# Second phase: an expert's remainder slot comes first, and small remainders run in column tiles, by branches

## The chip, the cores and the metric

The kernel runs on one core of a Trainium2 chip. The metric is the device time of one execution in microseconds (us). The engines are TensorE (PE), VectorE (DVE), ScalarE (ACT), GpSimd (POOL) and SyncE (SP), which issues most transfers.

## The reference

Three stages, all in float32. Attention in chunks and a first MLP with a rational activation give 3072 rows of 512 numbers; the third stage, which the change touches, sends each row to one of 8 experts:

```python
def _moe2_ref(x, w_gate, w1, w2):          # x [3072, 512], w1 [8, 512, 1024], w2 [8, 1024, 512]
    logits = x @ w_gate
    expert_idx = np.argmax(logits, axis=1)
    ...
    gate_w = probs[np.arange(N), expert_idx]
    for e in range(E):
        mask = expert_idx == e
        ...
        h = np.maximum(xe @ w1[e], 0.0)
        ye = h @ w2[e]
        out[mask] = gate_w[mask, None] * ye
```

The inputs come from a fixed seed. Counted with the reference, experts 0 to 7 get 0, 647, 638, 266, 0, 568, 0 and 953 tokens. In slots of 128 tokens that is 0, 6, 5, 3, 0, 5, 0 and 8 slots, 27 in all, and the remainders (the tokens beyond whole slots) are 7 for expert 1, 126 for expert 2, 10 for expert 3, 56 for expert 5 and 57 for expert 7.

## The kernel before

The first phase (attention, first MLP, gate, a rank of each token within its expert) takes some 690 us. The rows leave it sorted by expert into a DRAM buffer xs_d, each with its gate weight and its row number in the output.

The second phase works through the sorted rows in slots of 128 tokens. The expert with the most tokens comes first (slots 0 to 7, expert 7), then experts 1, 2, 3 and 5 from slots 8, 14, 19 and 22. For each slot j there are these steps, each with a function of its own:

- sl_load(j): SP loads the slot's 128 rows. Its address is in tBi, a table that plan_b1 computes on VectorE.
- weights1, weights2: SP loads the raw weights of the slot's expert into r1 and r2, in transfers with a condition, so that they move data only where the expert changes.
- sl_xt (L769 to L773): four transposes on PE; ACT copies the result as the high half (fp32r), VectorE computes the low half, and copies gate weight and row number to gid.
- sl_mm1 (L783): 24 matmuls of 128x128 by 128x512, since high and low halves of x and w1 make three products. They use w1h and w1l, converted from r1.
- sl_relu (L790): ACT, two halves.
- sl_ht (L798 to L801): eight transposes on PE, then high halves on ACT and low halves on VectorE.
- sl_mm2 (L807 to L809): 24 matmuls with w2h and w2l, converted from r2.
- sl_out (L818 to L824): VectorE multiplies by the gate weight and computes the row index, and GpSimd scatters the rows to the output.

hilo (L750, L751) converts one quarter of a weight matrix, with one operation on ACT and one on VectorE. on_change(j, piece) does it for four quarters behind a branch on both engines (a register load, L760, and a jump, L761), where slot j's expert is a new one. For slots 2 and 3 the conversions stand without a branch.

The program order of one turn j of the loop, which each engine follows for its part, is: weights1(j+2), ht(j), conversion of w2 for j; weights2(j+1), mm1(j+1), relu(j+1), xt(j+2), load(j+3), conversion of w1 for j+2; mm2(j), out(j). From slot 23 on, the turns stand within branches on the number of slots (nt, loaded at L1199, compared at L1192), which each engine loads once. There is no other scheduler: engines wait for each other by semaphores only.

Of the kernel before, what the change touches and what calls it, by code (L numbers as in the profile page):

```python
# [47 lines left out]
def build(ctx: ExitStack, tc, q, k, v, w_in, w_out, a, b, w_gate, w1, w2, cst, out):  # L48
# [6 lines left out]
    def T(shape, name, dt=F32):  # L55
        return sb.tile(shape, dt, name=name)
# [46 lines left out]
    r1 = [cut(AT, 1024 * i, 1024) for i in range(4)]  # L103
    r2 = [cut(AT, 4096, 1024), cut(AT, 5120, 1024), cut(elf, 0, 1024), cut(elf, 1024, 1024)]
    hs = cut(elf, 2048, 1024)
    sx = [cut(AT, 6144, XW), X2[:, 0], X2[:, 2]]
    ys = X2[:, 1, 0:D]
    wif = WI.rearrange("p f h c -> p f (h c)")
# [540 lines left out]
    sA = T([128, E], "sA")  # L649
    tAi = T([128, 2], "tAi", I32)  # L650
    tBi = T([128, 4], "tBi", I32)
    p_t = T([128, 4, E], "p_t")
# [5 lines left out]
    p_v = T([128, 4], "p_v")  # L658
    p_w = T([128, 4], "p_w")
    p_pr = cut(XT, 0, E * E, (E, E))  # L660
    p_lb = T([128, 32], "p_lb", BF16)
# [6 lines left out]
    def bc(x, n):  # L668
        return x.unsqueeze(1).to_broadcast([128, n, E])
# [10 lines left out]
    def plan_b1():  # L680
        vt = nc.vector
        vt.tensor_scalar(out=p_nbi, in0=p_cnt, scalar1=127.0, scalar2=None, op0=ALU.add)
        vt.tensor_scalar(out=p_nbi, in0=p_nbi, scalar1=7, scalar2=None, op0=ALU.logical_shift_right)
        vt.tensor_copy(out=p_nb, in_=p_nbi)
        vt.tensor_tensor(out=p_pr, in0=bc(p_nb, E), in1=lowm, op=ALU.mult)
        vt.tensor_reduce(out=p_en, in_=p_pr, op=ALU.add, axis=AX.X)
        vt.tensor_tensor(out=p_st, in0=p_en, in1=p_nb, op=ALU.subtract)
        vt.tensor_tensor(out=p_t[:, 0], in0=p_st, in1=sA, op=ALU.mult)
        vt.tensor_reduce(out=p_v[:, 0:1], in_=p_t[:, 0], op=ALU.add, axis=AX.X)
        vt.tensor_scalar(  # L690
            out=p_t[:, 1], in0=iota_e, scalar1=tA[:, 1:2], scalar2=p_en[:, E - 1:E], op0=ALU.is_lt, op1=ALU.mult
        )
# [44 lines left out]
    def sl_w1(w, kk):  # L737
        ex, ch = w
        src = w1[bass.ds(ex, 1), 128 * kk:128 * kk + 128, :].rearrange("o p f -> (o p) f")
        nc.sync.dma_start(out=r1[kk], in_=src, cond=ch, bounds_check=None)  # L740

    def sl_w2(w, kk):
        ex, ch = w
        src = w2[bass.ds(ex, 1), 256 * kk:256 * kk + 256, :].rearrange("o (a p) f -> p (o a) f", a=2)
        nc.sync.dma_start(
            out=r2[kk].rearrange("p (a f) -> p a f", a=2), in_=src, cond=ch, bounds_check=None
        )

    def hilo(src, hi, lo):
# [29 lines left out]
    def sl_mm1(j, kk):  # L779
        xh, xl = sxh[j % 2], sxl[j % 2]  # L780
        for m, (w, x) in enumerate(((w1h, xh), (w1l, xh), (w1h, xl))):
            for c in range(2):
# [2 lines left out]
                    start=(kk == 0 and m == 0), stop=(kk == 3 and m == 2),  # L785
                )

    def sl_relu(j):
# [24 lines left out]

    ixb = [T([128, 1], f"ix{i}", I32) for i in range(2)]

    def sl_out(j):
        g = gid[j % 4]
        nc.vector.tensor_scalar(out=ys, in0=ACC[j % 2], scalar1=g[:, 0:1], scalar2=None, op0=ALU.mult)  # L818
        ix = ixb[j % 2]
        if j < 2:  # L820
            nc.vector.tensor_copy(out=ix, in_=g[:, 1:2].bitcast(I32))
        else:
            nc.vector.tensor_tensor(out=ix, in0=g[:, 1:2].bitcast(I32), in1=skip[:, j:j + 1], op=ALU.add)  # L823
# [12 lines left out]
    KV.append(eb.tile([128, 2, 2, 2, 8, 64], F32, name="KV"))  # L836
    scratch = [ACC[2]]

    mid = ExitStack()

    def middle():
        early.close()
# [3 lines left out]

    def switch():
        mid.close()
        lp = ctx.enter_context(tc.tile_pool(name="lp", bufs=1))
# [243 lines left out]
    assert not todo  # L1093


    i = NCH - 1
    for kk in (2, 3):
        sl_w2(Z["a"], kk)
# [22 lines left out]
        sl_mm2(0, c)  # L1121
    sl_out(0)
    sl_load(2)

    def weights1(j):
        Z[j] = sl_w(j)
        for kk in range(4):
            sl_w1(Z[j], kk)

    def weights2(j):  # L1130
        for kk in range(4):
            sl_w2(Z[j], kk)

    weights1(2)
    sl_load(3)
    sl_ht(1)
    for kk in range(4):
# [11 lines left out]
    for kk in range(4):  # L1149
        sl_mm1(2, kk)  # L1150
        if kk < 3:
            sl_s1(kk)
    sl_relu(2)
    sl_xt(3, XB[2])
    sl_load(4)
    sl_s1(3)


    def head(j):
        if j + 2 < NS:  # L1160
            weights1(j + 2)
        sl_ht(j)
        if j > 2:
            on_change(j, sl_s2)

    def ahead(j):
        weights2(j + 1)
        for kk in range(4):
            sl_mm1(j + 1, kk)
        sl_relu(j + 1)  # L1170
        if j + 2 < NS:
            sl_xt(j + 2, XB[2])
            if j + 3 < NS:
                sl_load(j + 3)
            on_change(j + 2, sl_s1)

    def done_(j):
        for c in range(8):
            sl_mm2(j, c)
        sl_out(j)  # L1180

    for j in range(2, NS0 - 1):
# [19 lines left out]

def consts():
    import numpy as np
    c = np.zeros((128, CST_W), np.float32)
# [10 lines left out]
    c[:, 176:240] = (e[None, :] <= e[:, None]).reshape(-1)  # L1216
    c[:, 240:368] = p[None, :] > p[:, None]
    return c


# [53 lines left out]
```

## Time and profile before

| | before |
|---|---|
| median of 3 runs | 1050.24 us (1049.44 to 1052.48) |
| the profiled execution, its time | 1046.15 us |
| its span, first to last instruction | 1044.4 us |
| PE busy | 989.3 us (95%) |
| DVE busy | 702.2 us (67%) |
| ACT busy | 616.1 us (59%) |
| mean granted clock of TensorE | 0.984 |

The span is what the trace shows; the rows below are in us from its start. The granted clock is a share of full speed. Busy times leave out register loads, branches and the issuing of transfers.

### The profile page before, as it was taken

The page shows a single profiled execution, that of the slowest core. Times are in us where ns is not written, and L with a number is a line of the kernel's source. Part 1 is how long each engine was busy: PE and PEld are TensorE (multiplying, and loading weights), DVE is VectorE, ACT ScalarE, POOL GpSimd, SP SyncE. Part 2 cuts the span into 40 slices and gives each one's busy share as a digit, 9 for nine tenths or more (in the row PEclk, how much of TensorE's full clock was granted, in tenths as well). Part 3 has the DMA queues.
Part 4 walks back from the last instruction along what each step waited for, and adds up shares of the span by engine and source line. Part 5 has one row for each costly group of instructions (what it writes and reads, how often), then busy time and mean ns, then how long its engine had stood idle before and what let it go on. Part 6 is the DMA issues. An engine that isn't in the chain of part 4 may idle for free. (4 is left out here: it accounts for less than half of the span.)

```text
span 1044.4 us, 18684 instructions
## 1 busy us (share of the span) xinstructions
PE 989.3 (95%) x6427; PEld 845.7 (81%) x6427; DVE 702.2 (67%) x1283; ACT 616.1 (59%) x1118; POOL 384.8 (37%) x412
## 2 busy tenths in 40 slices
PE   4678998999999999999999999998999999999996
PEld 3567886888888898898898888886888888888885
DVE  6899998887877777877877878968324425244421
ACT  2557776786777777777777778764324325234321
POOL 2456664543663453463453464542101000000010
PEclk9889998999999999999999999999999999999999
DMA  9756323221221121121121022022124133154311
GB/s 252 225 176 173 131 81 107 56 61 52 82 71 62 61 82 51 51 82 51 52 81 52 21 102 71 1 72 71 42 76 168 46 122 113 52 178 145 113 42 38
DMA packets 48395, 93.09 MB, mean 89 GB/s; under 512 B 6935, under 2 KB 15391, under 8 KB 48288
## 3 DMA queue, kind: packets, MB, share of 16 engines
q1 hardware_dynamic: 43312, 78.46, 24.9%
q0 software_dynamic: 4080, 12.61, 3.2%
q8 instruction: 53, 0.87, 0.3%
q10 hardware_dynamic: 896, 0.72, 0.3%
q14 instruction: 54, 0.44, 0.1%
HBM read 169.32 MB, written 15.50 MB: 177 GB/s over the span
## 5 line engine op out<-in xcount | busy, mean ns | idle before, releaser
L379 PE MATMUL bank<-XX,WI 128*128 128x384 f32 x1536 | 303.0, 346 | 4.4 <-DVE EL L395 2.5
L379 PEld LDWEIGHTS bank<-XX,WI 128*128 128x128 f32 x1536 | 269.1, 191 | 17.9 <-DVE EL L395 5.0
L389 POOL TENSOR_TENSOR EL<-EL 128x384 f32<-128x384 f32 x128 | 133.5, 1043 | 234.0 <-ACT EL L388 233.9
L423 POOL TENSOR_TENSOR GG<-EL,GG 128x384 fp32r<-128x384 f32 x128 | 131.7, 1029 | 79.1 <-ACT GG L422 36.3
L783 PE MATMUL bank<-WI,XX 128*128 128x512 f32 x648 | 155.5, 395 | 2.8 <-ACT XX L771 1.7
L783 PEld LDWEIGHTS bank<-WI,XX 128*128 128x128 f32 x648 | 119.4, 188 | 28.2 <-ACT XX L771 1.8
L824 POOL DMA_INDIRECT out_dram<-X,ix x27 | 29.4, 1087 | 294.9 <-DVE ix L823 278.9
L431 PE MATMUL bank<-WOa,GG 128*128 128x512 f32 x288 | 115.7, 402 | 0.0
L432 PE MATMUL bank<-WOa,GG 128*128 128x512 f32 x288 | 114.8, 398 | 0.0
L415 DVE SCALAR_TENSOR_TENSOR EL<-EL,ab 128x384 f32<-128x384 f32 x114 | 107.8, 946 | 3.3
L422 ACT CAST GG<-EL 128x384 fp32r<-128x384 f32 x128 | 65.3, 510 | 67.1 <-DVE EL L415 48.6
L387 ACT ACTIVATE EL<-bank 128x384 f32<-128x384 f32 x128 | 62.1, 485 | 68.5 <-PE bank L379 67.6
L413 DVE SCALAR_TENSOR_TENSOR EL<-EL 128x384 f32<-128x384 f32 x114 | 64.2, 563 | 53.3 <-ACT EL L406 41.2
L800 ACT CAST XX<-bank 128x512 fp32r<-128x512 f32 x54 | 29.1, 591 | 108.9 <-PE bank L798 108.9
L388 ACT ACTIVATE EL<-EL,babs 128x384 f32<-128x384 f32 x128 | 90.8, 709 | 4.3
L772 DVE TENSOR_TENSOR XX<-bank,XX 128x512 fp32r<-128x512 f32 x28 | 19.4, 691 | 108.6 <-ACTq L761 85.0
L790 ACT ACTIVATE EL<-bank 128x512 f32<-128x512 f32 x54 | 29.3, 595 | 100.8 <-PE bank L783 99.6
L807 PE MATMUL bank<-WI,XX 128*128 128x512 f32 x216 | 87.0, 403 | 1.1 <-ACTq L761 0.9
L809 PE MATMUL bank<-WI,XX 128*128 128x512 f32 x216 | 84.7, 392 | 0.0
L808 PE MATMUL bank<-WI,XX 128*128 128x512 f32 x216 | 84.3, 390 | 0.3 <-DVEq L761 0.3
L399 DVE TENSOR_TENSOR EL<-EL,bank 128x384 f32<-128x384 f32 x128 | 70.1, 548 | 21.4 <-ACT EL L390 21.2
L390 ACT ACTIVATE EL<-bank,na 128x384 f32<-128x384 f32 x128 | 83.7, 654 | 0.0
(210 smaller groups left out, 1723.8 us busy)
## 6 DMA issues: line engine op xcount, KB each, us to landing
AT<-in_w_dram SPq DMA_DIRECT2D x164, 512.0 KB
EL<-in_w_dram SPq DMA_DIRECT2D x52, 512.0 KB
AT<-in_k_dram SPq DMA_DIRECT2D x80, 128.0 KB
AT<-in_v_dram SPq DMA_DIRECT2D x76, 128.0 KB
AT<-in_q_dram SPq DMA_DIRECT2D x23, 256.0 KB
X<-xs_d SPq DMA_DIRECT2D x18, 257.0 KB
AT<-in_w_out_dram SPq DMA_DIRECT2D x8, 512.0 KB
X<-in_w_out_dram SPq DMA_DIRECT2D x8, 512.0 KB
```

The costliest lines, as they stand in the source:

```text
L379: nc.tensor.matmul(h, lhsT=WI[:, f, w, 128 * kk:128 * kk + 128], rhs=xx(i)[:, x, kk, :], start=(m == 0), stop=(m == 11),)
L388: nc.scalar.activation(out=y, in_=u, func=AF.Identity, scale=babs[:, 1:2], bias=babs[:, 0:1])
L389: nc.gpsimd.tensor_tensor(out=y, in0=y, in1=u, op=ALU.mult)
L390: nc.scalar.activation(out=t, in_=h, func=AF.Identity, scale=na[:, 3:4], bias=na[:, 2:3])
L415: lambda: vt.scalar_tensor_tensor(out=t, in0=t, scalar=ab[:, 0:1], in1=w, op0=ALU.subtract, op1=ALU.mult),
L423: nc.gpsimd.tensor_tensor(out=gl, in0=g, in1=gh.bitcast(F32), op=ALU.subtract)
L431: nc.tensor.matmul(ACC[r], lhsT=gh[:, sl], rhs=wo(f, 0), start=first, stop=False)
L432: nc.tensor.matmul(ACC[r], lhsT=gh[:, sl], rhs=wo(f, 1), start=False, stop=False)
L783: nc.tensor.matmul(hbank(j)[c], lhsT=x[:, kk], rhs=w[kk][:, 512 * c:512 * c + 512], start=(kk == 0 and m == 0), stop=(kk == 3 and m == 2),)
L807: nc.tensor.matmul(y, lhsT=hh[:, c], rhs=wh, start=(c == 0), stop=False)
L808: nc.tensor.matmul(y, lhsT=hh[:, c], rhs=wl, start=False, stop=False)
L809: nc.tensor.matmul(y, lhsT=hl[:, c], rhs=wh, start=False, stop=(c == 7))
```

## The change

It puts the remainder slot of each expert first among the expert's slots. Its rows begin before the expert's first row, where the buffer has rows without tokens, so the tokens stand in the last of its 128 rows. plan_b1 computes a third table, tCi: 1 for a slot with at most 64 tokens, 2 for one with at most 32, 0 otherwise, and always 0 for an expert's last slot. For expert 7, whose slots 0 and 1 are fixed, the remainder takes slot 2.

For each slot from 2 on, PE, VectorE and GpSimd load the slot's class into a register (cls_load), all 29 loads at one place behind plan_b2. PE then takes one of three versions of each product by branches (by_size): the 24 matmuls as before; for 64, the plain fp32 product from the raw weights in two column tiles, each with half of the output's columns (8 matmuls of 512 columns in mm1, 16 of 256 in mm2); for 32, four column tiles (16 of 256, 32 of 128). A small matmul with a selection matrix (sel, L828) repeats gate weight and row number for every tile. Two more copies on ACT for every slot hold the fp32 operands (xf, hf). sl_out takes one of three versions as well, on VectorE and GpSimd. The conditional transfers of weights become transfers within a branch on SP. The conversions for slot 2 and its loads of weights are gone, and the conversion of w1 for slot 3 is now behind on_change.

```diff
+        if j > 1:
+            nc.scalar.copy(out=few[0], in_=pt[:, :, 64:128])
...
+    def mm1_few(j, n):
+        q, w = 128 // n, FE * n // 128
+        for kk in range(4):
+            for c in range(q):
+                x = nc.tensor.matmul(
+                    HB[0][n * c:n * c + n, 0:w], lhsT=few[0][:, kk, 64 - n:64], rhs=r1[kk][:, w * c:w * c + w],
+                    start=(kk == 0), stop=(kk == 3),
+                )
+                apart(x, (1, j + 1, kk))
+
+    def mm2_few(j, n):
+        y, g = ACC[j % 2], gid[j % 4]
+        q, w = 128 // n, D * n // 128
+        for f in range(8):
+            c, m = divmod(f, 8 // q)
+            for d in range(q):
+                o = 512 * (f % 2) + w * d
+                x = nc.tensor.matmul(
+                    y[n * d:n * d + n, 0:w], lhsT=few[1][:, m, n * c:n * c + n], rhs=r2[f // 2][:, o:o + w],
+                    start=(f == 0), stop=(f == 7),
+                )
+                apart(x, (2, j + 1, f // 2))
+        nc.tensor.matmul(y[:, 256:258], lhsT=sel[n], rhs=g, start=True, stop=True)
...
+    def by_size(flag, full, some):
+        with tc.If(flag < 1) as a_:
+            full()
+        with a_.Else():
+            with tc.If(flag < 2) as b_:
+                some(64)
+            with b_.Else():
+                some(32)
+
+    def cls_load(j):
+        cl[j] = nc.values_load(tCi[j:j + 1, 0:1], engines=[mybir.EngineType.PE], min_val=0, max_val=2)
+        co[j] = nc.values_load(
+            tCi[j:j + 1, 0:1], engines=[mybir.EngineType.DVE, mybir.EngineType.Pool], min_val=0, max_val=2
+        )
...
+            if j > 1 and c == 0:
+                nc.scalar.copy(out=few[1], in_=pt)
...
-    weights1(2)
     sl_load(3)
     sl_ht(1)
-    for kk in range(4):
-        sl_s1(kk)
-    weights2(2)
     weights1(3)
     for c in range(8):
         if c == XT2:
             sl_xt(2, XB[2])
         sl_mm2(1, c)
-        if c % 2:
-            sl_s2(c // 2)
     sl_out(1)
     plan_b2(ACC[2])
-    for kk in range(4):
-        sl_mm1(2, kk)
-        if kk < 3:
-            sl_s1(kk)
+    for j in range(2, NS):
+        cls_load(j)
+    mm1_by(2)
     sl_relu(2)
     sl_xt(3, XB[2])
     sl_load(4)
-    sl_s1(3)
+    on_change(3, sl_s1)
```

The order on PE at the start of the second phase, before: the last matmul of mm2(1), the matmul of plan_b2 (L716), and mm1(2) (L783), whose first matmuls wait for ACT's and VectorE's halves.

```order
L809 MATMUL bank_76<-WI,XX_68 128x512
L716 LDWEIGHTS oneb
L716 MATMUL bank_77<-p_lb,oneb 128x32
L783 MATMUL bank_78<-WI,XX_69 128x512 [waits Activation_49]
L783 MATMUL bank_79<-WI,XX_69 128x512
L783 MATMUL bank_78<-WI,XX_69 128x512 [waits DVE_49]
```

The same place after the change; L888 is mm2's last matmul, L724 that of plan_b2.

```order
L888 MATMUL bank_76<-WI,XX_68 128x512
L724 LDWEIGHTS oneb
L724 MATMUL bank_77<-p_lb,oneb 128x32
L842 TENSOR_LOAD tCi [waits DVE_49]
L842 ISA x2
L842 TENSOR_LOAD tCi
L842 ISA x2
```

So goes on a register load with two further register instructions, 29 times in all, before the branch of mm1(2).

Further on in PE's order, after the change, the end of mm1(2) with 24 matmuls, its two short versions (L810, 64 and 32 columns wide), and the transposes of slot 3 (L777). AT holds the raw weights r1.

```order
L793 MATMUL bank_79<-WI,XX_69 128x512
L833 UNCONDITIONAL_BRANCH
L836 COMPARE_AND_BRANCH
L810 MATMUL bank_78<-AT,xf 64x512 [waits DMAHW6_49,PE_49,Activation_49]
L810 MATMUL bank_78<-AT,xf 64x512 x3
L810 MATMUL bank_78<-AT,xf 64x512 [waits DMAHW0_49]
L810 MATMUL bank_78<-AT,xf 64x512
L810 MATMUL bank_78<-AT,xf 64x512 [waits DMAHW2_49]
L810 MATMUL bank_78<-AT,xf 64x512
L836 UNCONDITIONAL_BRANCH
L810 MATMUL bank_78<-AT,xf 32x256 [waits DMAHW6_49,PE_49,Activation_49]
L810 MATMUL bank_78<-AT,xf 32x256 x7
```

Before, the transposes followed mm1's last matmul directly; now a jump leads from the end of the full version over both short ones, and the short ones wait for transfers and for ACT, not for VectorE.

On VectorE, before, behind the output of slot 1 (L818, L821) and plan_b2's table skip (L717), come three conversions of w1 and then the low half of slot 3 (L772).

```order
L821 COPY ix_125<-gid_107 128x1
L717 TENSOR_SCALAR skip<-bank_77,cf 128x32 [waits PE_49]
L751 TENSOR_TENSOR WI<-AT,WI 128x1024 [waits DMAHW1_49,Activation_49]
L751 TENSOR_TENSOR WI<-AT,WI 128x1024 [waits DMAHW2_49,Activation_49]
L751 TENSOR_TENSOR WI<-AT,WI 128x1024 [waits DMAHW3_49,Activation_49]
L772 TENSOR_TENSOR XX_69<-bank_82,XX_69 128x512 [waits Activation_49]
```

After the change, the same place (L725 is skip).

```order
L914 COPY ix_126<-gid_107 128x1
L725 TENSOR_SCALAR skip<-bank_77,cf 128x32 [waits PE_49]
L843 TENSOR_LOAD tCi [waits DVE_49]
L843 ISA x2
L843 TENSOR_LOAD tCi
L843 ISA x2
```

Here too 29 loads follow each other, and the low half of slot 3 (L780) comes behind the last of them.

## Rows read from the trace of the kernel before

**Rows 1.** The page: engines' busy time; the group of the scatters.
```profile
PE 989.3 (95%) x6427; PEld 845.7 (81%) x6427; DVE 702.2 (67%) x1283; ACT 616.1 (59%) x1118; POOL 384.8 (37%) x412
...
L824 POOL DMA_INDIRECT out_dram<-X,ix x27 | 29.4, 1087 | 294.9 <-DVE ix L823 278.9
```

**Rows 2.** The chain that ended last, 880 to 906 us: start, us, what.
```profile
881.09 0.87 PE bank L798 x8
881.96 5.46 PE bank L783 x24
887.42 0.44 PE bank L769 x4
...
893.35 0.87 PE bank L798 x8
```

**Rows 3.** Waits of PE from 720 to 1040 us, largest two: total, times, longest.
```profile
PE bank L783 <- ACT XX L771: 1.7, 1, 1.7
PE bank L783 <- DVE XX L772: 1.1, 1, 1.1
```

**Rows 4.** Timeline of PE, gate product in tiles of 32 columns.
```profile
703.69 0.42 PE L467 MATMUL bank<-XT,wg 128*32 128x128 f32 x8
...
704.15 0.40 PE L467 MATMUL bank<-EL,wg 128*32 128x128 f32 x8
```

**Rows 5.** Lines L1199, L1192, L760: duration in ns min/median/max, first and last start.
```profile
L1199 PEldq TENSOR_LOAD <-tBi x1: 487/487/487, 987.3 to 987.3; - x1
...
L1192 PEldq COMPARE_BRANCH x5: 65/92/3324, 989.2 to 1032.2; - x5
...
L1192 PEldq COMPARE_BRANCH x1: 377/377/377, 1032.2 to 1032.2; - x1
...
L760 ACTq TENSOR_LOAD <-tBi x48: 275/282/472, 740.6 to 1029.3; - x48
```

**Rows 6.** Timeline of PE at the end of mm2(22).
```profile
991.17 0.39 PE L809 MATMUL bank<-WI,XX 128*128 128x512 f32 x1
```

**Rows 7.** Timeline of PE at the start of the second phase.
```profile
723.89 0.19 PE L716 MATMUL bank<-p_lb,oneb 128*128 128x32 bf16 x1
...
732.74 0.60 PE L769 MATMUL bank<-cf,AT 128*128 128x128 f32 x4
...
734.32 5.82 PE L783 MATMUL bank<-WI,XX 128*128 128x512 f32 x24
```

**Rows 8.** Line L722, SP's register loads, 717.8 to 719.1 us.
```profile
L722 SPq TENSOR_LOAD <-tBi x2: 267/271/275, 717.9 to 718.5; - x2
L722 SPq FUSED_REGOPS  x2: 152/152/152, 718.2 to 718.8; - x2
```

**Rows 9.** Line L760, VectorE's load of a branch's flag, 747 to 749 us.
```profile
L760 DVEq TENSOR_LOAD <-tBi x1: 310/310/310, 747.7 to 747.7; - x1
L760 DVEq FUSED_REGOPS  x1: 183/183/183, 748.1 to 748.1; - x1
L760 DVEq SEQ_ASSERT  x1: 23/23/23, 748.3 to 748.3; - x1
```

**Rows 10.** Windows: length, busy us of PE, PEld, DVE, ACT, POOL, clock, DMA, GB/s.
```profile
54.00:58.00 4.00, 1.84 (x7) 1.65 (x8) 3.90 (x8) 2.30 (x5) 3.51 (x3) 0.56 0.82 260
58.00:62.00 4.00, 4.00 (x14) 3.33 (x13) 3.86 (x8) 1.52 (x3) 0.72 (x1) 0.59 0.36 102
...
724.10:734.30 10.20, 7.44 (x36) 5.69 (x36) 10.20 (x13) 8.24 (x12) 2.96 (x1) 1.00 0.09 26
746.70:758.90 12.20, 12.20 (x62) 10.19 (x61) 2.83 (x7) 2.59 (x6) 0.97 (x1) 1.00 0.14 45
```

**Rows 11.** Timelines of PE and VectorE at slot 22's change of expert.
```profile
966.84 1.03 PE L798 MATMUL bank<-cf,EL 128*128 128x128 f32 x8
...
968.03 0.75 DVE L818 TENSOR_SCALAR X<-bank,gid 128x512 f32<-128x512 f32 x1
968.75 1.28 DVE L801 TENSOR_TENSOR XX<-bank,XX 128x512 fp32r<-128x512 f32 x2
```

More of the change, by code (lines that the diff above doesn't have):

```diff
@@ L32 @@
 CST_W = 368
+SEL_W = 256
 SEQ = (
@@ L651, in build @@
     tBi = T([128, 4], "tBi", I32)
-    p_t = T([128, 4, E], "p_t")
+    tCi = T([128, 1], "tCi", I32)
+    p_t = T([128, 5, E], "p_t")
     p_cnt = T([128, E], "p_cnt")
@@ L786, in sl_mm1, with apart, mm1_by, full @@
                 )
+    later = {}
+    def apart(x, key):
+        for y in later.get(key, []):
+            tc.declare_no_dep(
+                x.ins, y.ins, reason="a slot that reads the raw weights is never the last one of its expert"
+            )
[21 more added lines that the diff above has]
+        nc.tensor.matmul(y[:, 256:258], lhsT=sel[n], rhs=g, start=True, stop=True)
+    cl, co = {}, {}
+    def by_size(flag, full, some):
[10 more added lines that the diff above has]
+            tCi[j:j + 1, 0:1], engines=[mybir.EngineType.DVE, mybir.EngineType.Pool], min_val=0, max_val=2
+        )
+    def mm1_by(j):
+        def full():
+            for kk in range(4):
+                sl_mm1(j, kk)
+        by_size(cl[j], full, lambda n: mm1_few(j, n))
+    def mm2_by(j):
+        def full():
+            for c in range(8):
+                sl_mm2(j, c)
+        by_size(cl[j], full, lambda n: mm2_few(j, n))
+    def sl_gid(j):
+        g = gid[j % 4]
+        nc.vector.tensor_tensor(out=g[:, 1:2], in0=g[:, 1:2].bitcast(I32), in1=skip[:, j:j + 1], op=ALU.add)
     def sl_relu(j):
@@ L814, in build, with scatter, sl_out, full @@
     ixb = [T([128, 1], f"ix{i}", I32) for i in range(2)]
[L816 to L823, printed above, removed]
+    gq = T([128, 2], "gq")
+    part = {2: cf[:, 170:171], 4: cf[:, 171:172]}
+    def scatter(dst, ix, rows, src):
         nc.gpsimd.indirect_dma_start(
-            out=out,
+            out=dst,
             out_offset=bass.IndirectOffsetOnAxis(ap=ix, axis=0),
-            in_=ys,
+            in_=src,
             in_offset=None,
-            bounds_check=NT - 1,
+            bounds_check=rows - 1,
             oob_is_err=False,
         )
+    def sl_out(j):
+        g, y, ix = gid[j % 4], ACC[j % 2], ixb[j % 2]
+        vt = nc.vector
+        def full():
+            vt.tensor_scalar(out=ys, in0=y, scalar1=g[:, 0:1], scalar2=None, op0=ALU.mult)
+            vt.tensor_copy(out=ix, in_=g[:, 1:2].bitcast(I32) if j < 2 else g[:, 1:2])
+            scatter(out, ix, NT, ys)
+        def some(n):
+            q = 128 // n
+            w = D // q
+            vt.tensor_copy(out=gq, in_=y[:, 256:258])
+            vt.tensor_scalar(out=ys[:, 0:w], in0=y[:, 0:w], scalar1=gq[:, 0:1], scalar2=None, op0=ALU.mult)
+            vt.scalar_tensor_tensor(
+                out=ix, in0=gq[:, 1:2], scalar=float(q), in1=part[q],
+                op0=ALU.mult, op1=ALU.add,
+            )
+            scatter(out.rearrange("n (a b) -> (n a) b", a=q), ix, NT * q, ys[:, 0:w])
+        if j < 2:
+            full()
+        else:
+            by_size(co[j], full, some)
     early = ExitStack()
@@ L837, in build @@
     scratch = [ACC[2]]
-    mid = ExitStack()
+    mid, low = ExitStack(), ExitStack()
     def middle():
@@ L1093, in build @@
     assert not todo
+    low.close()
+    zp = ctx.enter_context(tc.tile_pool(name="zp", bufs=1))
+    few.append(zp.tile([128, 4, 64], F32, name="xf"))
+    few.append(zp.tile([128, 4, 128], F32, name="hf"))
     i = NCH - 1
@@ L1123, in build @@
     sl_load(2)
+    nc.sync.dma_start(out=XT[:, 128:384], in_=cst[:, CST_W:CST_W + SEL_W])
     def weights1(j):
         Z[j] = sl_w(j)
-        for kk in range(4):
-            sl_w1(Z[j], kk)
+        with tc.If(Z[j][1] > 0):
+            for kk in range(4):
+                later[1, j, kk] = [sl_w1(Z[j], kk)]
     def weights2(j):
-        for kk in range(4):
-            sl_w2(Z[j], kk)
-    weights1(2)
+        with tc.If(Z[j][1] > 0):
+            for kk in range(4):
+                later[2, j, kk] = [sl_w2(Z[j], kk)]
     sl_load(3)
     sl_ht(1)
-    for kk in range(4):
-        sl_s1(kk)
-    weights2(2)
     weights1(3)
@@ L1161, in head @@
             weights1(j + 2)
+        sl_gid(j)
         sl_ht(j)
@@ L1167, in ahead @@
         weights2(j + 1)
-        for kk in range(4):
-            sl_mm1(j + 1, kk)
+        mm1_by(j + 1)
         sl_relu(j + 1)
@@ L1177, in done_ @@
     def done_(j):
-        for c in range(8):
-            sl_mm2(j, c)
+        mm2_by(j)
         sl_out(j)
@@ L1216, in consts @@
     c[:, 176:240] = (e[None, :] <= e[:, None]).reshape(-1)
+    c[:, 170] = p // 64
+    c[:, 171] = p // 32
     c[:, 240:368] = p[None, :] > p[:, None]
+    for s, n in ((368, 64), (496, 32)):
+        c[:, s:s + 128] = (p[:, None] >= 128 - n) & (p[:, None] % n == p[None, :] % n)
     return c
```

41 lines of the change are left out of this document (23 added, 18 removed).

## The prediction

> **What bounds the kernel now.** I read the page's totals, the chain of waits, TensorE's (PE's) timeline where the second phase begins, its list of waits, and the register loads and jumps. The page [rows 1] has PE busy for 989.3 of 1044.4 us. The reader should see in the chain [rows 2] that it steps from PE to PE: one slot is ht (881.09), mm1 (5.46 us), xt (0.44 us), mm2, and ht again at 893.35, so a slot costs 12.26 us, of which mm2 is 12.26 − 0.87 − 5.46 − 0.44 = 5.49 us. From 720 to 1040 us PE's two largest waits [rows 3] are 1.7 and 1.1 us, in front of mm1(2) and inside it; the others are smaller. So in this phase time is won only by taking PE work out, and what stops PE's own queue is lost in full. The profiled execution took 1046.15 us, 1.75 more than its span; the median of the runs is 1050.24, 4.1 above it, and I move the sum over to the median unchanged.
>
> **Who is short.** By the token counts in the reference section, 4 of the 25 slots from slot 2 on run short: slots 8 and 19 (7 and 10 tokens) in tiles of 32, slots 2 and 22 (57 and 56) in tiles of 64. Slot 14 (126 tokens) stays full. The 27 scatters [rows 1] agree with the 27 slots.
>
> **What short products cost.** Four 128x128 transposes of fp32 take 0.44 us [rows 2], 0.11 us for one pass of 128 columns. The gate product of the first phase is fp32 in four tiles of 32 columns: eight records, two passes for each of four tiles, and three such groups start within 0.46 us of each other, 0.23 apart [rows 4]; one after the other they would need 0.87 us, so the four tiles run together. A 32-token product is four such groups of 256 columns (mm1) or eight of 128 (mm2): 8 x 0.22 (two passes of 0.11) = 1.75 us. A 64-token product is half of the output's columns again per tile: 3.5 us if two tiles run together, 7.0 if not. No row shows a tile of 64; the nearest is the tile of 32, so I take 3.5 and keep 7.0 as a rival. Savings: slots 8 and 19, (5.46 + 5.49 − 3.5 − 0.1 for the small gate product) = 7.4 each, 14.8; slot 22, 10.95 − 7.1 = 3.8; slot 2's mm2, 2.0. **Together −20.6 us.** Slot 2's mm1 goes with the next term.
>
> **The register loads.** Directly behind the matmul of plan_b2, PE's queue has 29 loads of tCi, each with two checks (L842 of the changed kernel), and only then mm1(2). PE's sequencer runs ahead of its array: its load at L1199 is made at 987.3, yet stands behind mm2(22) and so behind the matmul of 991.17 [rows 5, 6], 3.9 us. Behind mm2(1), whose end is the matmul of plan_b2 at 723.89 [rows 7], the loads can thus begin at about 720.2. Their pitch: SyncE's two stand 0.6 us apart (717.9, 718.5) [rows 8]; VectorE's are 0.310 + 0.183 + 0.023 us recorded, with starts 747.7, 748.1, 748.3, about 0.66 with the gaps [rows 9]. For PE there is one load, 487 ns, with a wait; ScalarE's worst load with a wait is 472 against 282 [rows 5, 9], so without one PE's is about 0.3. Bounds: below, SyncE's load and operation alone, 0.271 + 0.152 = 0.42; above, 0.487 + 0.183 + 0.023 and VectorE's gaps of 0.15, 0.85. I take VectorE's 0.66, whose load is the nearest to 0.3: 29 x 0.66 = 19.1 us, to 739.3 (0.42: 732.4; 0.85: 744.9). PE's array has nothing from 724.1 on, 15 us.
>
> The Trainium skill ("DMA: Bandwidth & Descriptors", Latency and other measured facts) puts a floor of some 600 ns under a tensor_load and says that loads are unrolled to amortize it. The trace has 271 to 310 ns on the load alone and 0.6 for load and checks together [rows 8, 9]; by the page's 0.6 plus the 0.2 of the checks the burst would be 23 us, near my upper bound.
>
> **What follows the burst.** After idle stretches the granted clock is near the lower of its two levels (1.2 of 2.4 GHz): 0.59 from 58 to 62 us although PE is busy throughout, behind four us of 46% busy at 0.56; with 2.8 us of pauses at 724 to 734 it stayed at 1.00 [rows 10]. After 15 us of nothing I let mm1(2) begin at half clock: 3.5 us become 5.5 (bounds 3.5 and 7.0), so xt(3) stands at 739.3 + 5.5 = 744.8 against 732.74 [rows 7]. VectorE does the same 29 loads from about 725.2, when plan_b2's result is there, to 744.4, then the low half of slot 3 (0.7 us): 746. ht(2) waits for relu(2), so mm1(3) begins near 746.7 against 734.32. **+12.4 us.** In it is that the 2.8 us of waits go, since the conversions of slot 2, of slot 3 and their places in ScalarE's and VectorE's queues are gone. If PE were done earlier, VectorE would still hold mm1(3) at about 745: the loads' lower bound wins only some 2 us. GpSimd's 29 loads stand ahead of scatter 2 only, which nothing waits for.
>
> **Smaller terms.** (a) 25 slots have two products each with a compare and a jump over the two short versions. A jump not taken is 92 ns, one over some 150 instructions 377 ns [rows 5], both on the sequencer, which is 3.9 us ahead in steady state and about 2 us at worst. I take +1 for 50 of them. The jumps that the conversions already put into PE's program left no wait in [rows 3]. (b) Before slots 8 and 19 the conversion of the new weights and the slot's output keep VectorE until 968.75, as at slot 22 [rows 11]; there L801 follows to 970.03 and mm1 of 5.46 us covers it. With mm1 of 1.75 the cover is 0.87 + 1.75 + 0.44 from 966.84, to 969.9, so mm2(7) waits for the low half and for ScalarE's extra copies: 1 us each, +2. At slot 22 the mm1 of 3.5 still covers. (c) The extra copies (some 0.9 us a slot on ScalarE), one small VectorE operation a slot, and the small plan operations cost nothing: ScalarE has 2.59 and VectorE 2.83 busy in 12.2 us [rows 10]. Without that cover they would be 25 us. (d) Weights by branch instead of conditional transfers are on SyncE, with a slot of 12 us to spare.
>
> **Sum:** −20.6 + 12.4 + 1 + 2 = −5.2 us: the span about 1039, the profiled execution about 1041, the median about **1045**.
>
> **Rivals.**
> *Two tiles of 64 do not run together* (slower). Slots 2 and 22 have four such products; each costs 7.0 in place of 3.5, so +14: 1059. It decides from 5.2 / 4 = 1.3 us more a product on. For it: no 64-wide row. Against: four tiles of 32 do [rows 4].
> *The loads are as slow as their upper bound.* PE's only load, at 487 ns, is longer than ScalarE's longest [rows 5]. 29 x 0.19 = +5.5: 1050.5, no change.
> *Loads cheap or the clock stays.* VectorE's burst then holds: −2, 1043.
> *Jumps stop PE* (slower). One jump over some 500 instructions took 3324 ns [rows 5]; less 2.2 us of run-ahead, 1.1 us would show at each of 25 to 50: +28 to +55, 1072 to 1100. Against: these jumps are over 50 to 100 instructions, and the one over 150 took 377 ns.
> The Trainium skill ("Runtime: NRT & Kernel Launch", Instruction fetch mechanics) says that a taken branch to a target outside the current window of two pages must fetch it first. The 3324 ns jump agrees; whether the shorter ones leave the window no row shows.
> *The branches always take the full version* (the change does not do what it says): −20.6 is gone, +15: 1065; the counts and the thresholds speak against it.
>
> **How the numbers follow.** Forecast 0.50; 64-wide tiles in turn 0.12; loads slow 0.18; loads cheap 0.08; jumps 0.09; never short 0.03. A measurement here tells 0.3% (3.2 us) from no change. The forecast's own range is 1041 to 1049, faster in 0.42 of its 0.50, same in the rest; loads cheap are faster (0.08); loads slow are same in 0.15, slower in 0.03; the other three are slower. Faster 0.50, same 0.23, slower 0.27. The range of 1038 to 1060 leaves out the jumps, the never-short case and a little at the lower end.
>
> **What will show it.** In the new trace: PE idle from 724 to about 739 with 29 loads at 0.66 us; a granted clock near 0.5 to 0.6 behind it; L810 and L823 in groups of 1.75 us (32 wide) and 3.5 us (64 wide); slots 8 and 19 some 7 us shorter; full slots still at 12.3 us. I am wrong if full slots are longer (jumps), if 64-wide groups take 7 us, or if the pitch of PE's loads is far from 0.66.

## The result, and the profile after

The changed kernel is slower: 1063.01 us median of 4 runs (1060.69 to 1064.74) against 1050.24 for three runs of the kernel before; the ratio of the means is 1.0116 with a 95% interval of 1.0082 to 1.0149. The range of the prediction ended at 1060, and its sign was wrong. (A fourth run of the kernel before, 1246.71 us, was disturbed and is left out.) The profiled execution took 1060.69 us with a span of 1058.9; before, 1046.15 and 1044.4. The two spans differ by 14.5 us, about 2 more than the medians do, and the accounts below are made on the spans.

From the page of the changed kernel, the busy times:

```profile
PE 979.3 (92%) x6531; PEld 827.8 (78%) x6531; DVE 692.6 (65%) x1304; ACT 628.7 (59%) x1157; POOL 382.1 (36%) x412
```

PE has 10 us less to do than in [rows 1], and yet the span is 14.5 us longer, so it stands idle for 24.5 us more. The short products are there, and more than they save has become waiting. PE's largest waits in the changed kernel, from 715 us on (released line and releaser: total us, times, longest), say where:

```profile
PE bank L810 <- issue: 17.8, 1, 17.8
PE bank L886 <- ACTq L769: 7.1, 4, 2.2
PE bank L887 <- DVEq L769: 2.8, 4, 0.8
PE bank L793 <- ACTq L769: 1.5, 2, 1.3
```

L810 is the short mm1, L793 the full one, L886 and L887 the first two matmuls of a full mm2; L769 is the branch around the conversions. The first line answers to the 2.8 us of [rows 3]. The other three are new, but for 1.2 us in front of the last mm2, which stood in the old kernel too. PE's timeline of the changed kernel at the start of the second phase:

```profile
723.95 0.19 PE L724 MATMUL bank<-p_lb,oneb 128*128 128x32 bf16 x1
741.92 6.48 PE L810 MATMUL bank<-AT,xf 128*64 128x512 f32 x16 [17.78 <-issue]
748.33 0.66 PE L777 MATMUL bank<-cf,AT 128*128 128x128 f32 x4
749.15 1.14 PE L875 MATMUL bank<-cf,EL 128*128 128x128 f32 x8 [0.16 <-ACT EL L867]
751.63 5.74 PE L793 MATMUL bank<-WI,XX 128*128 128x512 f32 x24 [1.33 <-ACTq L769]
```

This is the place that [rows 7] show in the old kernel. PE stands still for 17.8 us, its short mm1 then takes 6.4 us, and the transposes of slot 3 come at 748.33 instead of 732.74. The loads of PE's sequencer (line L842: duration in ns min/median/max, first and last start):

```profile
L842 PEldq TENSOR_LOAD <-tCi x29: 300/307/784, 720.5 to 740.7; - x29
L842 PEldq FUSED_REGOPS  x29: 146/146/167, 721.1 to 741.1; - x29
L842 PEldq SEQ_ASSERT  x29: 18/18/28, 721.4 to 741.3; - x29
```

They begin at 720.5, 3.4 us ahead of PE's last matmul before the pause (723.95), and stand (740.7 − 720.5) / 28 = 0.72 us apart.

The other place is where a short mm1 stands between a slot's ht and its mm2. PE at slot 8's mm1 (7 tokens, four tiles), then ScalarE and VectorE there:

```profile
810.75 1.03 PE L875 MATMUL bank<-cf,EL 128*128 128x128 f32 x8
811.71 1.93 PE L810 MATMUL bank<-AT,xf 128*32 128x256 f32 x32
813.58 0.66 PE L777 MATMUL bank<-cf,AT 128*128 128x128 f32 x4
816.39 0.51 PE L886 MATMUL bank<-WI,XX 128*128 128x512 f32 x1 [2.15 <-ACTq L769]
817.57 0.50 PE L887 MATMUL bank<-WI,XX 128*128 128x512 f32 x1 [0.68 <-DVEq L769]
```

```profile
811.87 0.57 ACT L877 CAST XX<-bank 128x512 fp32r<-128x512 f32 x1
815.21 0.59 ACT L880 COPY hf<-bank 128x512 f32<-128x512 f32 x1 [2.77 <-DVE XX L878]
815.70 0.59 ACT L877 CAST XX<-bank 128x512 fp32r<-128x512 f32 x1
```

```profile
809.16 4.63 DVE L759 TENSOR_TENSOR WI<-AT,WI 128x1024 fp32r<-128x1024 f32 x4 [1.72 <-ACT WI L758]
813.71 0.74 DVE L913 TENSOR_SCALAR X<-bank,gid 128x512 f32<-128x512 f32 x1
814.37 0.14 DVE L914 CAST ix<-gid 128x1 int32<-128x1 f32 x1
814.43 0.15 DVE L863 TENSOR_TENSOR gid<-gid,skip 128x1 f32<-128x1 int32 x1
814.50 0.68 DVE L878 TENSOR_TENSOR XX<-bank,XX 128x512 fp32r<-128x512 f32 x1
```

They are read together from the bottom. VectorE has conversions until 813.7 and comes to the low half (L878) at 814.5. ScalarE's new copy hf (L880) waits 2.77 us for that low half, although it reads only the bank that the low half reads too; behind it in ScalarE's queue waits the cast of the second half (L877), and behind that the branch, whose end releases mm2's first matmul. PE stands still for 2.15 us, and 0.68 more for VectorE. The same pair of waits stands in front of slots 19 (2.2 and 0.8 us), 22 (0.5 and 0.8) and in the last slot, 26 (2.2 and 0.5), where no mm1 stands between.

What the pauses do to the clock, by windows (columns as in [rows 10]):

```profile
741.90:748.30 6.40, 6.38 (x16) 1.89 (x16) 0.00 (x0) 0.00 (x0) 0.00 (x0) 0.55 0.01 3
816.30:820.30 4.00, 3.23 (x13) 2.46 (x14) 1.46 (x3) 1.94 (x4) 0.00 (x0) 1.00 0.53 182
949.00:953.00 4.00, 3.19 (x8) 2.49 (x8) 1.01 (x3) 1.63 (x4) 0.00 (x0) 0.51 0.46 159
1044.00:1048.00 4.00, 4.00 (x11) 3.15 (x12) 0.00 (x0) 0.00 (x0) 0.00 (x0) 0.58 0.08 12
```

The granted clock is near the lower level behind the loads, behind slot 19's pause and behind the last; behind slot 8's pause, nearly as long as slot 19's (2.83 us against 3.03), it stayed at 1.00.

The distance from one ht to the next, taken from PE's timelines of all kernels (the start of L875, in the old kernel L798), is the best measure of the rest. Each row of this table is one profiled execution; ht(1) stands at times up to 4.6 us apart (716.10 in e4, 720.67 in e3), which the differences leave out.

| us between starts of ht | 1 to 3 | 7 to 8 | 8 to 9 | 18 to 19 | 19 to 20 | 21 to 22 | 22 to 23 | 1 to 26 |
|---|---|---|---|---|---|---|---|---|
| before | 29.61 | 12.28 | 12.27 | 12.28 | 12.28 | 12.28 | 12.28 | 311.92 |
| after | 45.25 | 12.17 | 9.00 | 15.16 | 9.01 | 12.36 | 10.72 | 323.35 |

From ht(7) to ht(8) there is a short mm1, from ht(8) to ht(9) a short mm2. The short mm2 gave 3.3 us at slots 8 and 19 and 1.6 at slot 22; the short mm1 gave nothing at slots 8 and 22 and lost 2.9 at slot 19. The turns between full slots are at 12.28, as before, but for two: 9 to 10 took 12.78 and 20 to 21 took 12.65. They come behind the short mm2 of slots 8 and 19, and in them mm1 begins 1.27 and 1.14 us after ht begins, against about 0.8 in the other turns; at 833.19, mm1(10), PE waits 0.20 us for ScalarE's branch. Behind ht(26) come the other 3.1 us.

### The profile page after: what moved, and what is told of

Read it like the earlier page. It is cut to its first block, busy times and chain, and to the rows that moved or that the text cites. A ratio compares the mean times of both kernels' runs of the same rounds, so it can differ in the third digit from the quotient of the medians.

```text
span 1058.9 us, 18911 instructions
## 1 busy us (share of the span) xinstructions
PE 979.3 (92%) x6531; PEld 827.8 (78%) x6531; DVE 692.6 (65%) x1304; ACT 628.7 (59%) x1157; POOL 382.1 (36%) x412
## 4 chain that ended last, share of the span: by engine, by line
PE 50%; issue 24%; DMA 12%; DVE 7%; ACT 4%; POOLq 1%; POOL 1%; SPq 0%; another core or an unknown queue 0%; DVEq 0%; ACTq 0%
PE bank L382 21%; DMA out_dram<-X,ix 8%; PE bank L434 7%; PE bank L435 7%; PE bank L438 7%; PE bank L251 2%; PE bank L301 2%; DVE EL L418 1%; DMA AT<-in_v_dram 1%; DVE EL L417 1%; PE bank L320 1%; POOLq L843 1%; PE bank L288 1%; PE bank L462 1%; DVE bank L637 1%
## 5 line engine op out<-in xcount | busy, mean ns | idle before, releaser
L899 POOL DMA_INDIRECT out_dram<-X,ix x27 | 26.3, 973 | 312.5 <-DVE gid L863 292.4
L793 PE MATMUL bank<-WI,XX 128*128 128x512 f32 x552 | 132.3, 394 | 1.6 <-ACTq L769 1.5
L793 PEld LDWEIGHTS bank<-WI,XX 128*128 128x128 f32 x552 | 101.8, 188 | 23.6 <-ACTq L769 2.3
L434 PE MATMUL bank<-WOa,GG 128*128 128x512 f32 x288 | 115.6, 402 | 0.0
L435 PE MATMUL bank<-WOa,GG 128*128 128x512 f32 x288 | 114.8, 398 | 0.0
L780 DVE TENSOR_TENSOR XX<-bank,XX 128x512 fp32r<-128x512 f32 x28 | 19.3, 690 | 105.8 <-ACT XX L779 105.8
L438 PE MATMUL bank<-WOa,GG 128*128 128x512 f32 x288 | 82.8, 395 | 0.0
L886 PE MATMUL bank<-WI,XX 128*128 128x512 f32 x184 | 75.6, 411 | 7.3 <-ACTq L769 7.1
L408 ACT ACTIVATE EL<-EL,c 128x384 f32<-128x384 f32 x128 | 79.1, 618 | 3.3 <-POOL EL L392 3.3
L398 DVE SCALAR_TENSOR_TENSOR EL<-EL,ab,bank 128x384 f32<-128x384 f32 x128 | 77.9, 608 | 1.7
```

Of the source, the lines that this page charges most:

```text
L398: poly = lambda: vt.scalar_tensor_tensor(out=t, in0=t, scalar=ab[:, 1:2], in1=h, op0=ALU.subtract, op1=ALU.mult)
L408: nc.scalar.activation(out=rb, in_=y, func=AF.Ln, bias=c1)
L434: nc.tensor.matmul(ACC[r], lhsT=gh[:, sl], rhs=wo(f, 0), start=first, stop=False)
L435: nc.tensor.matmul(ACC[r], lhsT=gh[:, sl], rhs=wo(f, 1), start=False, stop=False)
L438: nc.tensor.matmul(ACC[r], lhsT=gl[:, sl], rhs=wo(f, 0), start=False, stop=stop)
L793: nc.tensor.matmul(hbank(j)[c], lhsT=x[:, kk], rhs=w[kk][:, 512 * c:512 * c + 512], start=(kk == 0 and m == 0), stop=(kk == 3 and m == 2),)
```

## The experiments

Theory A, formed from these traces: the loss has two parts. One is the row of 29 loads with the half clock behind it. The other is the chain ScalarE, VectorE, ScalarE, VectorE around the copies xf and hf, which shows wherever mm1 is short or missing. Its rivals were that the loads alone lose (B), that loads cost wherever they stand (C), and that jumps and copies cost in every full slot (D).

### e1: hf ahead of the low half

```diff
             nc.scalar.copy(out=hh[:, s], in_=pt)
-            nc.vector.tensor_tensor(out=hl[:, s], in0=pt, in1=hh.bitcast(F32)[:, s], op=ALU.subtract)
             if j > 1 and c == 0:
                 nc.scalar.copy(out=few[1], in_=pt)
+            nc.vector.tensor_tensor(out=hl[:, s], in0=pt, in1=hh.bitcast(F32)[:, s], op=ALU.subtract)
```

> The changed kernel with one edit: ScalarE's copy hf stands ahead of VectorE's low half of ht, so it no longer waits for VectorE, and the cast of the second half behind it no longer does either. Theory A (the loss has two parts: 15.8 us at the burst of register loads, and the chain ScalarE, VectorE, ScalarE, VectorE around hf, which shows wherever mm1 is short or absent, with the half-clock stretches that its pauses bring): the waits of mm2 on ScalarE in front of slots 8, 19, 22 and 26 (7.1 us together) shrink to below 3, VectorE's conversions still hold some 1.5 us at slots 8 and 19, the stretches at 0.51 and 0.70 of the clock go, 5 to 10 us less than the changed kernel, 1053 to 1058. Rival B (the burst alone is the loss, the waits behind short products are VectorE's conversions and not hf): at most 1.5 us less, 1061 or more.

Measured: 1052.41 us, 1.001 of before (0.999 to 1.0031), so some 10 us less than the changed kernel from the order of two lines, and 0.6 below the range given. PE's largest waits:

```profile
PE bank L810 <- issue: 17.7, 1, 17.7
PE bank L887 <- DVEq L769: 3.6, 3, 1.5
PE bank L886 <- ACTq L769: 1.4, 1, 1.4
PE bank L793 <- ACTq L769: 1.3, 1, 1.3
```

The waits on ScalarE fell from 7.1 to 1.4 us; 1.4 to 1.5 us of waiting for VectorE remain at slots 8 and 19, where PE had waited for 2.83 and 3.03 us in all, and the granted clock behind them is 1.00 (816.6 to 820.6 and 947.3 to 951.3 us). ht(18) to ht(19) is 10.56 instead of 15.16: 1.5 us of the gain is the shorter wait, the other 3.1 go with the clock. The turns 9 to 10 and 20 to 21 are 12.34. Rival B is out.

Not all of the difference belongs to the edit: ht(1) to ht(3) is 1.25 us shorter too, though the waits there are as before (17.7 and 1.3 us). mm1(2) took 5.29 us instead of 6.48, at a granted clock of 0.68 (743.86 to 749.06 us) instead of 0.55.

### e2: the loads taken apart

```diff
+    cls_pe(2)
+    cls_pe(3)
     weights1(3)
...
-    for j in range(2, NS):
-        cls_load(j)
...
             on_change(j, sl_s2)
+        cls_out(j)
...
             sl_xt(j + 2, XB[2])
+            if j > 1:
+                cls_pe(j + 2)
```

cls_pe and cls_out are the two halves of cls_load.

> The changed kernel with the 29 register loads taken apart: PE loads a slot's class two turns ahead, VectorE and GpSimd load it within the slot's own turn. Theory A: PE's wait of 17.8 us and the half clock behind it go, ht(2) stands near 729 to 731 instead of 749, and one load of 0.72 us a slot is hidden by the run-ahead of PE's sequencer: 18 to 21 us less than the changed kernel, 1042 to 1045. Rival C (each load costs PE its 0.7 us wherever it stands, since the sequencer has no time to spare between the waits and jumps): 25 x 0.7 = 17 us come back, no faster than 1057. In both the waits in front of slots 8, 19, 22 and 26 stay.

Measured: 1044.58 us, 0.9937 of before (0.9911 to 0.9962). ht(1) to ht(3) is 24.78 us, 20.5 less than in the changed kernel; full turns stay at 12.28 but for the two named above (12.79 and 12.53), and PE waits for no row of loads any more: a load that its sequencer makes ahead of its array costs nothing here. Rival C is out. The waits in front of slots 8, 19, 22 and 26 are as in the changed kernel (L888 and L889 are mm2's first two matmuls):

```profile
PE bank L888 <- ACTq L769: 7.1, 4, 2.2
PE bank L889 <- DVEq L769: 2.8, 4, 0.8
```

Here the clock fell at slot 8 as well (0.57 from 800.2 to 804.2 us; that turn took 15.09).

### e3: both

The edits of e1 and e2 in one kernel.

> Both edits together: hf ahead of VectorE's low half, and the loads taken apart. Theory A: the two gains add, 24 to 30 us less than the changed kernel, 1034 to 1039, and so 11 to 16 us faster than before. Rival B: as with the loads alone, 1042 to 1045. Rival C: 1050 or more.

Measured: 1032.31 us, 0.9822 of before (0.9779 to 0.9864), 1.7 us below the range given. From ht(1) to ht(26) it takes 294.59 us: e1 saved 9.1 of the changed kernel's 323.35, e2 18.8, both 28.8. The two parts are independent and add up within 1 us.

### e4: never short

```diff
-        vt.tensor_tensor(out=tCi, in0=p_v[:, 0:1], in1=p_v[:, 4:5], op=ALU.mult)
+        vt.tensor_scalar(out=tCi, in0=p_v[:, 0:1], scalar1=p_v[:, 4:5], scalar2=0.0, op0=ALU.mult, op1=ALU.mult)
```

> The changed kernel with the class multiplied by zero: every slot runs the full version by its branches, all loads, copies and jumps stay. Theory A: burst 15.8 us, mm1(2) in full partly at half clock some 3 us more, the wait of the last mm2 with its half clock 3 us: 20 to 23 us above before, 1069 to 1073; the other turns last 12.28 us as before, and no wait stands in front of slots 8, 19 and 22. Rival D (jumps and extra copies cost in each full slot): turns longer than 12.35 us, 1076 or more.

Measured: 1067.05 us, 1.0162 of before (1.0118 to 1.0205), 2 us below the range that was given. ht(1) to ht(3) is 46.86 us, 17.3 above before; all turns behind are 12.25 to 12.37, and only the last mm2 waits, 2.2 and 0.5 us. So loads, jumps and copies without the short products cost these two things and nothing in full slots: rival D is out.

### e5 and e6: one engine's loads apart, the others' in a row

Of e2's edits, e5 has those of PE alone and e6 those of VectorE and GpSimd alone; the other half of the loads stays behind plan_b2.

> The changed kernel with only PE's 29 loads taken apart; VectorE's and GpSimd's stay in a row behind plan_b2. Theory A with the step of the prediction that VectorE's row alone holds mm1(3): PE comes to mm1(3) some 19 us after ht(1) as with all loads apart, VectorE's loads end 28 us after ht(1), the low half of slot 3 and the branch behind them some 1.5 us later, so PE waits about 10 us for VectorE there, with half clock behind it: 10 to 13 us over the kernel with all loads apart, 1055 to 1058. Rival E (VectorE's row is off the path): 1043 to 1046.

Measured: 1061.94 us, 1.0089 of before (1.0064 to 1.0114): 4 us over the range given, and nearly what the changed kernel takes. PE is early at ht(2) and then waits 16.2 us:

```profile
733.19 1.14 PE L877 MATMUL bank<-cf,EL 128*128 128x128 f32 x8 [0.17 <-ACT EL L869]
750.55 7.66 PE L793 MATMUL bank<-WI,XX 128*128 128x512 f32 x24 [16.21 <-ACTq L769]
```

VectorE's and ScalarE's timelines of e5 show for what:

```profile
749.01 0.69 DVE L780 TENSOR_TENSOR XX<-bank,XX 128x512 fp32r<-128x512 f32 x1 [19.19 <-issue]
...
749.74 0.37 ACT L782 COPY xf<-bank 128x256 f32<-128x256 f32 x1 [15.63 <-DVE XX L780]
```

VectorE's loads hold the low half of slot 3 until 749.0, the copy xf waits for the low half, ScalarE's branch stands behind the copy, and mm1(3) waits for the branch. (e9, below, takes the wait of xf away.) So VectorE's row, with GpSimd's beside it, is enough to lose some 17 us against e2, and e6 shows the same of PE's; they do not add, as they lie side by side. Rival E is out. GpSimd's row by itself was not tried.

> The changed kernel with only VectorE's and GpSimd's loads taken apart; PE's stay in a row. Theory A: PE's own row ends later than VectorE's, so PE's wait of 17.7 us and the half clock behind it stay: 1060 to 1063, as the changed kernel. Rival F (the loads of three engines slow each other down): PE's pitch falls from 0.72 us and the wait to 14 us or less, 1057 or less.

Measured: 1064.46 us, 1.0113 of before (1.0088 to 1.0139), near the changed kernel's result and 1.5 us over the range given. PE waits 17.65 us, its loads are still 20.0 us from first to last (744.8 − 724.8), against 20.2 with the other engines' rows beside them. So the engines do not slow each other's loads by much, and rival F is out.

### e8: the loads in the kernel before

```diff
     plan_b2(ACC[2])
+    for j in range(2, NS):
+        nc.values_load(tBi[j:j + 1, 2:3], engines=[mybir.EngineType.PE], min_val=0, max_val=1)
+        nc.values_load(
+            tBi[j:j + 1, 2:3], engines=[mybir.EngineType.DVE, mybir.EngineType.Pool], min_val=0, max_val=1
+        )
```

> The kernel before with nothing but 29 register loads on PE, VectorE and GpSimd behind plan_b2, whose values nothing uses. Theory A: PE idle for 17.7 us in place of its 2.8 us of waits, and mm1(2) partly at half clock, 2 to 3 us: 16 to 18 us above before, 1067 to 1070. Rival B2 (in the old order the conversions hide part of it, or the loads cost only through what the new kernel has behind them): under 12 us above before.

Measured: 1065.75 us, 1.0134 of before (1.0115 to 1.0154), 14 us more, where 16 to 18 were expected. In the trace, ht(1) to ht(3) grew by 16.7 us, all turns behind are 12.28, and PE stands still for 16.8 us in front of mm1(2):

```profile
745.03 7.37 PE L783 MATMUL bank<-WI,XX 128*128 128x512 f32 x24 [16.80 <-issue]
```

The loads alone make the old kernel about as slow as the changed one.

### e7: the flag early

e3, and the flag of the branches around the conversions is loaded once for each slot, ahead of relu:

```diff
     def on_change(j, piece):
-        flag = nc.values_load(tBi[j:j + 1, 2:3], engines=CVT, min_val=0, max_val=1)
-        with tc.If(flag > 0):
+        with tc.If(fl[j] > 0):
...
         mm1_by(j + 1)
+        if j + 2 < NS:
+            flag_load(j + 2)
         sl_relu(j + 1)
```

> Both edits (hf ahead, loads apart), and the flag of the branches around the conversions is loaded once for each slot on ScalarE and VectorE, ahead of relu, and not twice right before each branch. Theory A (mm2's and mm1's waits on the branch's end come from the load that stands before it): the waits of 1.33 us at mm1(3), 1.4 and 1.5 at slots 8 and 19 and 1.35 at the last mm2 fall by 0.3 to 0.7 us each, 1 to 3 us less than with both edits, 1029 to 1031 beside 1032.3. Rival G (the branch itself, or the copies before it, is what they wait for): no change, 1032 to 1033.

Measured: 1030.1 us, 0.9804 of before (0.9785 to 0.9824). In the trace mm1(3) waits 1.00 (1.33 in e3), slots 8 and 19 wait 1.08 and 1.15 (1.42 and 1.50), the last mm2 still 1.35, though it was expected to fall too; ht(1) to ht(26) takes 292.76, 1.8 less than e3. Where they fell, the waits fell by 0.33 to 0.35, the least that was expected; another 0.55 us of the 1.8 is a wait for slot 2's rows (a DMA) that e3's trace has at 726.44 and e7's has not. The medians alone, 2.2 us apart with ranges that overlap, would not settle it.

### e9 and e10: xf ahead, and the output late

e9 adds to e7 the same exchange for xf:

```diff
+        if j > 1:
+            nc.scalar.copy(out=few[0], in_=pt[:, :, 64:128])
         nc.vector.tensor_tensor(out=l, in0=pt, in1=h.bitcast(F32), op=ALU.subtract)
-        if j > 1:
-            nc.scalar.copy(out=few[0], in_=pt[:, :, 64:128])
```

> The kernel with hf ahead, loads apart and the flag early, and ScalarE's copy xf ahead of VectorE's low half of xt, so that it waits for VectorE no more. Theory A: PE's wait of 1.0 us at mm1(3) for ScalarE's branch end falls to 0.4 or less; elsewhere xt has 5 us of cover, nothing changes: 0.5 to 1 us less, 1029 to 1030, at the edge of what a measurement tells. Rival H (the 0.4 us that the low half comes later delays mm1 or mm2): the same or 1 us more.

Measured: 1028.3 us, 0.9777 of before (0.9753 to 0.9802), the fastest kernel of the study, though its interval overlaps those of e7 and e10. PE's largest waits in the whole second phase:

```profile
PE bank L892 <- ACTq L773: 1.4, 1, 1.4
PE bank L893 <- DVEq L773: 0.6, 3, 0.3
PE bank L892 <- ACT XX L883: 0.2, 1, 0.2
```

The wait at mm1(3) is gone, as expected. Not expected: the waits at slots 8 and 19 fell too, from 1.08 and 1.15 to 0.16. The conversions say why. In e7 VectorE stands idle for 1.37 us between its part of xt and its first conversion, since ScalarE's first conversion stands behind xf; in e9 for 0.17 (first lines e7's, then e9's):

```profile
788.72 0.69 DVE L784 TENSOR_TENSOR XX<-bank,XX 128x512 fp32r<-128x512 f32 x1 [5.18 <-ACT XX L783]
789.32 0.16 DVE L787 COPY gid<-X 128x2 f32<-128x2 f32 x1
790.85 4.63 DVE L759 TENSOR_TENSOR WI<-AT,WI 128x1024 fp32r<-128x1024 f32 x4 [1.37 <-ACT WI L758]
```

```profile
787.55 4.63 DVE L759 TENSOR_TENSOR WI<-AT,WI 128x1024 fp32r<-128x1024 f32 x4 [0.17 <-ACT WI L758]
```

e10 adds to e9 that sl_out(j) stands behind ht(j+1) in the program.

```diff
         sl_ht(j)
+        if j > 2:
+            sl_out(j - 1)
...
         mm2_by(j)
-        sl_out(j)
```

> The same, and VectorE's output of a slot (0.75 and 0.14 us) and its scatter stand behind the low halves of the next slot's ht. Theory A (what is left of the waits at slots 8 and 19, 1.08 and 1.15 us, is VectorE's queue: four conversions and this output ahead of the low halves): they fall to 0.3 us or less, 1.5 us less than with xf ahead alone, the end stays within 0.5 us: 1027 to 1029. Rival I (the waits are those for new weights or for ScalarE): they stay, no gain.

Measured: 1030.1 us, 0.9799 of before (0.9774 to 0.9825): no gain over e9, and the 1.5 us less that were expected did not come. It was made for the 1.1 us that e9 had just removed; at slots 8 and 19 e10 has 9.26 and 9.21 us where e9 has 9.22 and 9.25. At the end it loses: the second matmul of the last mm2 waits 1.05 us for VectorE (0.28 in e9).

| us between starts of ht | 1 to 3 | 7 to 8 | 8 to 9 | 18 to 19 | 19 to 20 | 21 to 22 | 22 to 23 | 1 to 26 |
|---|---|---|---|---|---|---|---|---|
| e1 | 44.00 | 10.50 | 9.54 | 10.56 | 9.01 | 10.57 | 11.12 | 314.22 |
| e2 | 24.78 | 15.09 | 9.01 | 13.98 | 9.01 | 12.37 | 10.73 | 304.53 |
| e3 | 25.32 | 10.50 | 9.00 | 10.56 | 9.01 | 10.55 | 10.73 | 294.59 |
| e9 | 23.75 | 9.22 | 9.00 | 9.25 | 9.01 | 10.52 | 10.72 | 290.38 |

Two turns of e1 are 0.5 and 0.4 us longer than in the other kernels (8 to 9 and 22 to 23); its trace names no engine that PE waited for there.

## Why the prediction was wrong

The sum was −5.2 us; the span grew by 14.5, a difference of 19.7. By places:

| place | forecast | measured | difference |
|---|---|---|---|
| loads, slots 2 and 3 (ht(1) to ht(3)) | +10.4 | +15.6 | +5.2 |
| slots 8 and 19 | −12.8 | −3.8 | +9.0 |
| slot 22 | −3.8 | −1.5 | +2.3 |
| other turns (forecast: jumps) | +1.0 | +1.0 | 0.0 |
| behind ht(26) | 0 | +3.1 | +3.1 |

The forecasts are the prediction's terms put together by place: 12.4 less 2.0 for slot 2's mm2; twice 7.4, less the 2 of (b). The measured values are the differences of the first table. That the row of other turns agrees is chance: the forecast was for jumps in every turn, but 0.9 of the measured 1.0 lie in the turns 9 to 10 and 20 to 21, and e1 takes most of that away by the order of the copies. With all jumps and no short product (e4) the turns from ht(3) to ht(26) take 0.2 us more than before.

**The register loads: right in mechanism, too small.** PE did idle behind plan_b2, the loads did begin 3.4 us early (3.9 was forecast), and behind them the clock was near half (0.55). Three sizes were off. The pitch was 0.72 us and not the 0.66 taken from VectorE's single load, so the row ended 2 us later. mm1(2) took 6.4 us, near half clock from end to end, not 5.5. And mm1(3) waited another 1.33 us for ScalarE's branch, which stands behind xf, a wait that I had not seen. That VectorE's own row would hold mm1(3) by itself was right (e5), and so was the estimate that cheaper loads on PE would win only some 2 us (e5: 2.7 from ht(1) to ht(3)). The Trainium skill ("DMA: Bandwidth & Descriptors", Latency and other measured facts) has some 600 ns as the floor of a tensor_load. The trace does not agree: the load alone is 307 ns here, and loads with their two checks stand 0.72 us apart. By the page, the estimate for the row (23 us) was 2 us too high.

**Short products: right.** The short mm1 took 1.87 us (811.71 to 813.58) in tiles of 32 and 3.6 in tiles of 64 (980.69 to 984.28), mm2 with the gate product 2.1 and 3.9, each 0.1 to 0.3 more than forecast. So two tiles of 64 run together, and that rival is out. Slot 14 ran full.

**Term (c), and (b) with it, was the step that failed.** Term (c) put the extra copies at nothing, because ScalarE has 2.6 us of work in a slot of 12.2. Only (b) had a wait for them, 1 us each at slots 8 and 19, and took slot 22 as covered. The order shows what I left out: the copy hf stands between the two halves' casts and behind VectorE's low half, and it waits for VectorE. That put a chain through both engines' queues between ht and mm2. A full mm1 of 5.46 us covers it, and so full turns did not change (e4); where mm1 is short the cover goes, and PE waits for 2.8 to 3.0 us at slots 8 and 19, 1.3 at slot 22. In the last slot there never was cover. Term (b), "1 us each, +2", saw VectorE's conversions and the copies there, but neither that a copy itself waits for VectorE nor what followed the pause at slot 19 and in the last slot: near half clock for several us. e1 shows the size of both together: of its 9.1 us from ht(1) to ht(26), the 7.9 behind ht(3) come from exchanging two lines. With the loads apart and all of these waits cut down (e9), slots 8 and 19 take 12.6 us less than before, where the forecast had 12.8. That the copies do wait for the low half is in the rows. With the order exchanged it is VectorE's low half that waits for the copy hf, as here in e9 (L886 is the low half, L885 hf):

```profile
801.37 1.29 DVE L886 TENSOR_TENSOR XX<-bank,XX 128x512 fp32r<-128x512 f32 x2 [0.60 <-ACT hf L885]
```

So the order in the program decides which of the two waits; why two operations that only read the same bank are not made side by side, these runs leave open.

**The rivals.** None of the slower ones was what happened, and none of them priced the chain of copies. Jumps cost nothing visible: ahead of mm1(8) one took 1.99 us on PE's sequencer (from 808.8) and left no gap in PE's work, and with all jumps in place full turns stayed at 12.28 us (e4). The longest, 4.9 us from 1046.0, stands behind the last mm2, where PE has nothing more to do. The Trainium skill ("Runtime: NRT & Kernel Launch", Instruction fetch mechanics) lets a taken branch out of the window wait for a fetch; whether these two jumps did, no row shows. The slow-loads rival is the one that came nearest, with 0.72 between my 0.66 and its 0.85.

## What to carry to other kernels

A wait that cannot be seen today because a long operation covers it comes out when that operation is made short; so for every product that is shortened, list all that stands between the producer and the next product in each engine's queue, copies and register loads included, and ask of each what it waits for. Load registers a turn ahead of their use, one at a time: a row of 29 in front of a tensor product cost 17 us here, and the same loads spread out cost nothing. An extra copy of a bank that another engine reads too is better placed ahead of that reading than behind it: that order alone was worth some 8 us here. A place at the end of the copying engine's queue was not tried. With these edits, and the branches' flags loaded early, the idea pays: 1028.3 us, 2.2% under the kernel before.

## What the runs showed of the hardware

- A register load on PE with its two checks takes 0.72 us in a row of 29 (307, 146 and 18 ns recorded), VectorE's 0.70 (743.7 − 724.2 over 28), GpSimd's load without checks 0.40 (736.1 − 725.0 over 28).
- Two column tiles of 64 run side by side in fp32: 8 matmuls of 512 columns take 3.6 us; in four column tiles of 32, 16 matmuls of 256 columns take 1.87.
- Pauses of nearly the same length do not always bring the lower clock: 2.15 and 0.68 us at slot 8 left it at 1.00 in the changed kernel and brought 0.57 in e2; at slot 19, with 2.2 and 0.8 us, 0.51 and 0.74. With the first of the two waits gone (e1, 1.4 to 1.5 us left) it stayed at 1.00 in both places. What else decides it, these runs leave open.
